# 64-row score tiles for the first head group, a new load order and a new last block in an attention and feed-forward kernel

## The chip, the cores and the metric

One core of one Trainium2 chip. The metric is the time of one execution in device microseconds. An execution more than 1.5% above the fastest of the same kernel is called slow here, and two kernels are compared by their fast executions alone, with a 95% interval. This matters more than usual: the kernel before has two times, some 921 and some 940 us, in about equal shares. Its executions near 921 us are called undisturbed below, those near 940 us disturbed.

## The reference

An input x (2048 rows, 512 columns, bfloat16) goes through attention with 32 heads of 16 elements and through a gated feed-forward block with 1792 hidden columns. A sigmoid gate for each row mixes the two.

```
g = sigmoid((x * gate_w).sum(-1, keepdims=True))
a = softmax(q @ k.T * 16 ** -0.5) @ v      # for each of 32 heads, then @ wo
b = (silu(x @ w_gate) * (x @ w_up)) @ w_down
out = g * a + (1 - g) * b
```

## The kernel before

Scores are kept transposed: 128 keys on the partitions, 512 queries along the row. Four heads make a group; there are 8 groups, 4 query blocks and 16 key tiles, so 2048 score tiles. Nearly all go in pairs to one 128x1024 exponential on ScalarE (902 of these); 244 single tiles get an approximate exponential on VectorE. "Pair n" below is the n-th exponential on ScalarE: a ruler that does not depend on time.

The four heads of a group lie at partitions 0, 32, 64 and 96. In group 0 a score is one 32-row matmul in its own row strip of the array. In the other groups it is a 64-row matmul over a strip of two heads, and the other head's rows of the query tile are zero:

```python
    HEADS = (0, 2, 1, 3)

    def score(ps, b):
        n, j = b // 4, HEADS[b % 4]
        (qb, g), kt = UNIT[n // KT], n % KT
        if g == 0:
            r = slice(32 * j, 32 * j + 32)
            mm(ps, lhsT=kaug[r, g, kt * P:(kt + 1) * P], rhs=q0[qb][r, :], start=True, stop=True,
               tile_position=(32 * j, 0))
        else:
            r = slice(64 * (j // 2), 64 * (j // 2) + 64)
            mm(ps, lhsT=kaug[r, g, kt * P:(kt + 1) * P], rhs=get_qx(qb, g // 2)[r, j % 2, g % 2, :],
               start=True, stop=True, tile_position=(64 * (j // 2), 0))
```

The query block of group 0 is made like this: a copy, the absolute value, a bound (one matmul), and its addition. `later(t, f)` and `plan.dve` do not run on the chip: they are the builder's estimates of when VectorE will be done, and by them it decides in which order the instructions are emitted.

```python
        def end():
            vec.tensor_copy(out=q0[qb], in_=st["p"][:, :])
            m_free(plan.dve)
            aq = work.tile([P, QBW], BF16, tag="aq", name="aq", bufs=4)
            vec.tensor_scalar(out=aq[:, :].bitcast(U16), in0=q0[qb].bitcast(U16), scalar1=0x7FFF, scalar2=None,
                              op0=ALU.bitwise_and)
            plan.dve += 0.33
            st["aq"] = aq

        def bound():
            st["b"] = m_tile("bp")
            mm(st["b"][:, :], lhsT=kneg0, rhs=st["aq"][:, :], start=True, stop=True)
            spend("F", 1)
            later(0.6, end_b)

        def end_b():
            vec.tensor_tensor(out=q0[qb], in0=q0[qb], in1=st["b"][:, :], op=ALU.add)
            m_free(plan.dve)
```

At the start the transposed input comes on SyncE's queue and the weights on ScalarE's. VectorE fills seven groups of `kaug` with ones before it can make the first key bound:

```python
    for c0 in (0, D):
        nc.scalar.dma_start(out=wqk[:, :, c0 + 64:c0 + D],
                            in_=A_wqkv[:, c0 + 64:c0 + D].rearrange("(dc p) c -> p dc c", p=P))
    # ... (cut)
    nc.scalar.dma_start(out=wv, in_=A_wqkv[:, 2 * D:3 * D].rearrange("(dc p) c -> p dc c", p=P))
    # ... (cut)
    for g in range(1, G):
        nc.vector.memset(kaug[:, g, :], 1.0)
```

At the end both halves of the last product wait for the last group's sums, and the four output tiles share two buffers (`opool` has `bufs=2`):

```python
    for w in range(2):
        for tq in range(TQ):
            cs = slice(tq * P, (tq + 1) * P)
            mm(a_ps[tq][:, 0:D], lhsT=(osbs[un - 1], on_l)[w][:, cs], rhs=wo_l[:, w, :],
               start=(w == 0), stop=(w == 1))
    for tq in range(TQ):
        store(qb * TQ + tq, a_ps[tq], acc[0][:, tq, :])
```

## Time and profile before

| | us |
|---|---|
| three timed executions | 921.09, 940.65, 945.73 (median 940.65) |
| profiled execution | 947.81, span 946.1, a slow one |
| ScalarE busy in the span | 876.4 (93%) |
| TensorE busy in the span | 856.0 (90%) |

The page of the kernel before cuts the span into 40 slices of 23.7 us. A digit is a share in tenths; PEclk is the clock granted to TensorE.

```profile
ACT  1989966899999999999999999999999999999994
PEclk9999855899999999999999999999999999999998
```

The two dips lie in the same slices. The timeline of the kernel before (start, duration, engine, idle before and who ended it):

```profile
57.38 0.40 PE L158 MATMUL s_t<-on,kaug 32*128 32x512 bf16 x4
57.61 0.37 PE L158 MATMUL d_t<-on,kaug 32*128 32x512 bf16 x1
57.90 1.94 ACT L161 ACTIVATE e_t<-s_t 128x1024 bf16<-128x1024 f32 x2 [0.57 <-PE s_t L158]
57.92 1.04 PE L158 MATMUL vp<-rb,xT 128*128 128x512 bf16 x4
```

Behind four value sums, for which it waited on VectorE's copy of a value tile, TensorE sends five scores in a row. From the first score to the next full matmul pass 57.92 - 57.38 = 0.54 us. ScalarE waits at its end for these scores: 0.57 us. Here TensorE is on the path, though it idles beforehand.

### The profile page before, as it was taken

How to read it: one execution, taken by the hardware profiler on the slowest of the kernel's cores; microseconds unless marked ns; L12 is line 12 of the kernel's file. 1: busy time of each engine (PE TensorE's matmuls, PEld its weight loads, DVE VectorE, ACT ScalarE, POOL GpSimd, SP SyncE). 2: the span in 40 equal slices, each digit the busy share in tenths (PEclk: the TensorE clock that was granted, in tenths of full speed). 3: DMA queues.
4: the chain of work that ended last, by engine and by line, in shares of the span. 5: the costliest groups of instructions: out<-in, count | busy, mean ns of one | idle time of the engine just before them, and what ended most of it. 6: DMA issues, size and time to landing. Idle time of an engine off the chain costs nothing.

```text
span 946.1 us, 14215 instructions
## 1 busy us (share of the span) xinstructions
PE 856.0 (90%) x5165; PEld 217.0 (23%) x5165; DVE 737.5 (78%) x1018; ACT 876.4 (93%) x967; POOL 8.9 (1%) x30
## 2 busy tenths in 40 slices
PE   4889999999999999999999998999999999889985
PEld 1222211222222222222222222222222222222221
DVE  7259865789888887987878778888778798887782
ACT  1989966899999999999999999999999999999994
POOL 3000000000000000000000000000000000000000
PEclk9999855899999999999999999999999999999998
DMA  9400102102110111111001112110001121100000
GB/s 182 112 4 19 30 18 40 35 21 53 27 29 7 35 37 41 53 45 33 7 4 29 37 33 53 46 38 13 4 12 32 39 56 35 29 9 4 23 1 22
DMA packets 87534, 31.97 MB, mean 34 GB/s; under 512 B 75120, under 2 KB 87016, under 8 KB 87464
## 3 DMA queue, kind: packets, MB, share of 16 engines
q1 hardware_dynamic: 84824, 29.50, 13.7%
q10 hardware_dynamic: 2640, 1.57, 0.7%
q8 instruction: 40, 0.66, 0.3%
q14 instruction: 30, 0.25, 0.1%
HBM read 20.83 MB, written 2.34 MB: 24 GB/s over the span
## 4 chain that ended last, share of the span: by engine, by line
PE 44%; ACT 38%; issue 10%; DVE 6%; DMA 2%; SPq 1%; ACTq 0%; DVEq 0%
ACT e_t L161 36%; PE s_t L158 17%; PE o_ps L158 9%; PE gp L158 4%; PE dps L158 3%; PE d_t L158 3%; PE up L158 2%; DVE y_t L167 2%; ACT th L161 2%; PE kp L158 2%; PE qp L158 1%; DMA xT<-in_A_x_dram 1%; PE a_ps L158 1%; PE vp L158 1%; DVE u_t L167 1%
## 5 line engine op out<-in xcount | busy, mean ns | idle before, releaser
L161 ACT ACTIVATE e_t<-s_t 128x1024 bf16<-128x1024 f32 x902 | 849.7, 1041 | 35.4 <-PE s_t L158 31.5
L158 PE MATMUL s_t<-qx,kaug 64*128 64x512 bf16 x1572 | 332.2, 386 | 54.9 <-ACT e_t L161 51.7
L167 DVE TENSOR_SCALAR y_t<-d_t 128x512 uint16<-128x512 f32 x244 | 167.6, 687 | 100.0 <-PE d_t L158 97.8
L158 PE MATMUL o_ps<-e_t,vaug 128*32 128x512 bf16 x1804 | 198.0, 398 | 4.6 <-DVE vaug L167 3.9
L158 PEld LDWEIGHTS <-kaug 64*128 64x128 bf16 (+1 forms) x2048 | 100.6, 93 | 358.3 <-issue 353.7
L167 DVE TENSOR_TENSOR u_t<-u_t,z_t 128x2048 f16<-128x2048 f16 x122 | 148.9, 1220 | 2.3
L158 PEld LDWEIGHTS <-vaug 128*32 128x32 bf16 x2048 | 53.3, 94 | 192.0 <-issue 183.4
L158 PE MATMUL d_t<-qx,kaug 64*128 64x512 bf16 x220 | 83.7, 380 | 0.0
L167 DVE TENSOR_TENSOR y_t<-y_t,u_t 128x2048 uint16<-128x2048 uint16 x61 | 74.4, 1219 | 0.8
L158 PE MATMUL gp<-xT,wg 128*128 128x512 bf16 x224 | 71.2, 401 | 0.0
L158 PE MATMUL up<-xT,wu 128*128 128x512 bf16 x224 | 70.0, 399 | 0.0
L158 PE MATMUL dps<-wd_t,mt 128*128 128x512 bf16 x224 | 67.6, 384 | 0.0
L158 PE MATMUL s_t<-on,kaug 32*128 32x512 bf16 x232 | 49.5, 443 | 3.8 <-ACT e_t L161 3.5
L167 DVE SCALAR_TENSOR_TENSOR mt<-gs,up 128x512 bf16<-128x512 bf16 x56 | 38.2, 682 | 14.6 <-PE up L158 13.9
L167 DVE SCALAR_TENSOR_TENSOR gs<-th,gp 128x512 bf16<-128x512 bf16 x56 | 38.1, 680 | 9.1 <-ACT th L161 8.8
L167 DVE TENSOR_SCALAR u_t<-z_t 128x2048 f16<-128x2048 uint16 x61 | 42.1, 691 | 1.5
L167 DVE TENSOR_SCALAR z_t<-y_t 128x2048 uint16<-128x2048 uint16 x61 | 41.9, 687 | 0.8
L167 DVE TENSOR_SCALAR u_t<-u_t 128x2048 f16<-128x2048 f16 x61 | 41.8, 686 | 0.7
L167 DVE TENSOR_SCALAR y_t<-y_t 128x2048 uint16<-128x2048 uint16 x61 | 41.8, 686 | 0.5
L161 ACT ACTIVATE th<-gp 128x512 bf16<-128x512 f32 x56 | 34.2, 610 | 0.3 <-PE gp L158 0.3
L167 DVE CAST osb<-o_ps 128x512 bf16<-128x512 f32 x32 | 21.9, 685 | 13.7 <-PE o_ps L158 13.5
L158 PEld LDWEIGHTS <-mt 128*128 128x128 bf16 x260 | 16.5, 100 | 52.6 <-issue 45.8
(89 smaller groups left out, 331.5 us busy)
## 6 DMA issues: line engine op xcount, KB each, us to landing
wg<-in_B_w_gate_dram SPq DMA_DIRECT2D x56, 128.0 KB
wu<-in_B_w_up_dram SPq DMA_DIRECT2D x56, 128.0 KB
out_dram<-o_t SPq DMA_DIRECT2D x16, 128.0 KB
on<-osb SPq DMA_DIRECT2D x120, 16.0 KB
rb<-rr SPq DMA_DIRECT2D x15, 128.0 KB
wd_t<-in_B_w_down_dram SPq DMA_DIRECT2D x1, 1792.0 KB
qx<-qst SPq DMA_DIRECT2D x112, 16.0 KB
kaug<-on SPq DMA_DIRECT2D x20, 64.0 KB
```

The costliest lines, as they stand in the source:

```text
L158: ordered(nc.tensor.matmul(*args, **kw))
L161: ordered(nc.scalar.activation(*args, **kw))
L167: return lambda *a, **kw: ordered(f(*a, **kw))
```

## The change

Its intent: give group 0 the 64-row form of the other groups; keep the weights from competing with the transposed input; shorten the last block. The 64-row form needs two query tiles with alternate heads zeroed (`vsel`), so VectorE passes over each block twice, and the bound takes two matmuls. The tiles borrow parts of other tiles (`qx`, `on_t`, `mt`). The order of emission has a new cap, at most two blocks of vector exponentials in flight (`y_live`), and a rule on late blocks; the planning charges were raised as well. The core of the diff:

```diff
-    for c0 in (0, D):
-        nc.scalar.dma_start(out=wqk[:, :, c0 + 64:c0 + D], ...)
-    nc.scalar.dma_start(out=wv, ...)
+    nc.sync.dma_start(out=wv, ...)          # behind the transposes on the same queue
+    for c0 in (D, 0):
+        nc.sync.dma_start(out=wqk[:, :, c0 + 64:c0 + D], ...)
 ... query block of group 0
-                    later(0.6, end)
+                    later(1.2, end)
-            vec.tensor_copy(out=q0[qb], in_=st["p"][:, :])
+            for v in range(2):
+                vec.tensor_scalar(out=q0[qb][:, v, :], in0=st["p"][:, :], scalar1=vsel[:, v:v + 1], scalar2=None,
+                                  op0=ALU.mult)
-            plan.dve += 0.33
+            plan.dve += 0.46
-            mm(st["b"][:, :], lhsT=kneg0, rhs=st["aq"][:, :], start=True, stop=True)
-            spend("F", 1)
-            later(0.6, end_b)
+            for v in range(2):
+                mm(st["b"][:, :], lhsT=kneg0, rhs=st["aq"][:, v, :], start=(v == 0), stop=(v == 1))
+            spend("F", 2)
+            later(1.2, end_b)
-            vec.tensor_tensor(out=q0[qb], in0=q0[qb], in1=st["b"][:, :], op=ALU.add)
+            for v in range(2):
+                vec.scalar_tensor_tensor(out=q0[qb][:, v, :], in0=st["b"][:, :], scalar=vsel[:, v:v + 1],
+                                         in1=q0[qb][:, v, :], op0=ALU.mult, op1=ALU.add)
 ... score(): the 32-row branch goes
+        r = slice(64 * (j // 2), 64 * (j // 2) + 64)
+        q = q0[qb][r, j % 2, :] if g == 0 else get_qx(qb, g // 2)[r, j % 2, g % 2, :]
 ... rules of emission
-        if late and (now is None or late[0][0] <= now):
+        if late and late[0][1][0] // (4 * KT) == closed and (now is None or late[0][0] <= now):
-            d_ok = dq and dq[0] <= pq[0][-1] + 2 and ...
+            d_ok = (vcur or y_live[0] < 2) and dq and dq[0] <= pq[0][-1] + 2 and ...
 ... last block
+    last_mm(0, osbs[un - 1])                # ahead of the wait for the last group
     dt = ps_d.tile([P, QBW], F32, tag="d", name="dt")
 ... (cut)
+    last_mm(1, on_l)
     for tq in range(TQ):
-        store(qb * TQ + tq, a_ps[tq], acc[0][:, tq, :])
+        store(qb * TQ + tq, a_ps[tq], acc[0][:, tq, :], mt[:, tq, :])
```

## The prediction

> **What bounds the kernel now.** I read the page's clock row first, then the busy times by stretch, the waits inside the odd stretch, the groups, and last the two ends in order of time.
>
> The three timed runs of before are 921.09, 940.65 and 945.73 us, so the median is not the kernel's only time. The clock row has a dip near the start; busy times by stretch (span; then PE, weight loads, VectorE, ScalarE, GpSimd as us and count; clock; DMA share; GB/s) show it:
>
> ```profile
> 100.00:105.00 5.00, 5.00 (x31) 1.44 (x30) 4.96 (x8) 5.00 (x7) 0.00 (x0) 1.00 0.24 53
> 105.00:110.00 5.00, 3.97 (x36) 1.32 (x34) 4.86 (x8) 5.00 (x7) 0.00 (x0) 0.98 0.12 28
> 110.00:115.00 5.00, 5.00 (x20) 0.81 (x19) 2.76 (x5) 3.61 (x5) 0.00 (x0) 0.50 0.00 1
> ...
> 170.00:175.00 5.00, 5.00 (x17) 0.74 (x15) 1.73 (x3) 3.47 (x4) 0.00 (x0) 0.54 0.11 26
> 175.00:180.00 5.00, 5.00 (x34) 1.19 (x33) 4.97 (x8) 4.56 (x7) 0.00 (x0) 1.00 0.24 54
> ```
>
> Outside that stretch ScalarE is the bound: 98.5 of every 100 us from 200 to 900 us. Inside it TensorE has half its clock, is busy all the time, and ScalarE starves. The waits from 109.7 to 174.6 us (total, times, longest):
>
> ```profile
> ACT e_t L161 <- PE s_t L158: 20.9, 28, 1.9
> ```
>
> The page's groups say what runs there: 232 first-group score tiles of 32 rows, slower in the mean than the 64-row ones (386 ns):
>
> ```profile
> L161 ACT ACTIVATE e_t<-s_t 128x1024 bf16<-128x1024 f32 x902 | 849.7, 1041 | 35.4 <-PE s_t L158 31.5
> L158 PE MATMUL s_t<-on,kaug 32*128 32x512 bf16 x232 | 49.5, 443 | 3.8 <-ACT e_t L161 3.5
> ```
>
> So 20.9 of ScalarE's 35.4 us of idle before exponentials lie in the half-clock stretch. The profiled run (947.81 us) is a slow one; 940.65 - 921.09 = 19.6 and 945.73 - 921.09 = 24.6 say that the 921.09 run simply missed the dip.
>
> The start, in order of time (start, duration, engine, idle before and its releaser):
>
> ```profile
> 15.51 1.86 PE L158 MATMUL kp<-xT,mt 128*128 128x512 bf16 x4 [6.75 <-DMA xT<-in_A_x_dram]
> 17.43 1.76 DVE L222 MEMSET kaug<- 128x2048 bf16 x1 [0.38 <-issue]
> 20.90 1.23 DVE L167 TENSOR_REDUCE kpart<-kp 128x1 f32<-128x1024 f32 x1 [1.68 <-PE kp L158]
> 24.94 1.08 ACT L161 ACTIVATE vaug<-vp 128x512 bf16<-128x512 f32 x2
> 25.58 1.02 PE L158 MATMUL vp<-rb,xT 128*128 128x512 bf16 x4 [2.21 <-ACT vaug L161]
> 28.21 17.52 ACT L161 ACTIVATE e_t<-s_t 128x1024 bf16<-128x1024 f32 x19
> ```
>
> TensorE waits 6.75 us for transposed input, but VectorE has memsets until 17.43 + 1.76 = 19.19 us and reaches the reduction only behind them. The end:
>
> ```profile
> 939.27 1.41 DVE L167 SCALAR_TENSOR_TENSOR o_t<-al,gval,kaug 128x512 bf16<-128x512 f32 x2 [1.78 <-PE al L158]
> 941.90 1.41 DVE L167 SCALAR_TENSOR_TENSOR o_t<-a_l,gval,kaug 128x512 bf16<-128x512 f32 x2 [1.22 <-DMA out_dram<-o_t]
> ```
>
> The third and fourth output tiles wait 1.22 us for the first stores to free their buffer.
>
> [...] the half-clock stretch is 64.853 us, 19 windows of 3.413 us. [...]TensorE was busy 2.80 of the 3.4 us before the drop, and fully busy while held down[...]. I counted, for each window on the trace's own grid, rows x columns x streamed elements of the matmuls that start in it, over 128 x 128 x 8192[...]. A 512-element 32-row score, or a 128-row 32-column value matmul, is 1/4 x 1/16 = 0.0156; a 64-row score 0.031; a full one 0.0625. The window that ends at the drop (106.3 to 109.7) has 8 scores, 8 value matmuls, one full one and small ones: 0.125 + 0.125 + 0.0625 + 0.005 = 0.317, the lowest of all in the stage. The held windows have 0.27 to 0.375 and the one before release 0.406. From 175 to 932 us the lowest is 0.406 and the clock never drops; at 932 us a window of 0.127 drops it. One threshold between 0.375 and 0.406 fits every transition. That is my estimate from the trace[...]. [...] here a pair of scores takes about 0.39 us in either shape, as only two run side by side, so 64 rows should cost no time.
>
> **The change part by part.**
> 1. 64-row first group. Recounting the bad window with 64 rows gives 0.317 + 8 x 0.0156 = 0.442, above the threshold. The changed instruction order also spreads that spot: by the same count over four successive score pairs (4 x 0.92 us), before has a minimum of 0.207 at pair 78, after 0.438 anywhere in the first 250 pairs. So the drop should go in every run: -20.9 us of starvation, less about 1 us of ordinary idle, -20 us against a slow run, nothing against the 921.09 run.
> 2. Its price. Three more 128-row bound matmuls, 3 x 0.22 = 0.7 us of TensorE. On VectorE each of three later query blocks goes from one 0.69 us copy and 0.29 us mask to two 0.69 us products and a mask twice as wide (about 0.46), and from one 0.69 us addition to two: 3 x (0.86 + 0.69) = 4.7 us, spread over 28 to 75 us. VectorE waited 19.4 us for value tiles there, so it is hidden: 0. The first block's halves are separate instructions and the first score pair waits for the first half only: 0 to 0.7.
> 3. Weights behind the input. Input packets moved 1800 per 2 us when alone and about 560 beside the weights; 8192 packets at 900 per us need 9 us, so the last quarter lands near 12 rather than 19.6 us and the projections end near 14.5. But the memsets remain: VectorE starts its first reduction at about 19.9, against 20.90: -0.9. Against that, TensorE now idles from about 17 to 24 us, over two windows, and resumes at half clock: four value matmuls and the bound on the path cost 5 x 0.21 = 1.1 us more, and one or two windows of slow start perhaps 1 us. Net +1.2 (-1 to +3).
> 4. The end. Four matmuls of the earlier group go ahead of the wait for the last group's sums, into 0.79 us in which TensorE idles: the first output tile can start about 1.2 us earlier; the stores from own tiles drop the 1.22 us wait. Together -2.4.
> 5. The emission rules (a cap on vector-computed blocks in flight) reorder but do not add: after has the same 902 exponentials and, in its order, the same runs of four value-tile matmuls ahead of value sums that cost ScalarE 3.3 us at 52 to 63 us. 0 +/- 3.
>
> Sum: 921.1 + 1.2 - 2.4 = 919.9. The profiled run less its excess gives 946.1 - 20 = 926 instead; since that run was also 4.6 us above the mean of the two slow timed ones, it points to about 921 and so the same. I take 920.
>
> **The rivals.**
> - The clock still drops, elsewhere. Against: 64-row windows before never fell under 0.406 until the end; for: 0.406 is only just above what held the clock, and the reordered stages are new. A drop with 64-row tiles would recover in a few windows, each about 3.4 x 0.3 = 1 us: 922 to 926. If it stays as long as before, 940.
> - Activity is not what I count, and the drop comes from the short pauses of TensorE just before it (0.6 us of 3.4) alone. Then the rearranged order decides; the time would be 920 or 940 by chance.
> - The start gains in full: if the memsets do not hold the reduction, the input's 7 us come through: 914. Against it stands the row that ends at 19.19.
> - The doubled VectorE work delays the query blocks and stalls scores near 40 to 70 us, where ScalarE already lost 3.3 us: 923 to 925.
>
> **Range and chances.** With the drop gone the base is 921 +/- 3; start and end add -4 to +1, order +/- 3: 913 to 928 for 8 in 10. Two per cent under 940.65 is 921.84, so a predicted 920 sits barely past it: faster 0.57, same 0.41 (nearly certain if only the undisturbed run of before is compared), slower 0.02.
>
> **What would show it.** The clock row should be full from about 30 us to the end; no 32-row group; score matmuls near 385 ns throughout; ScalarE's idle before exponentials near 15 us in place of 35.4; the input landed by 13 us, yet the first exponential still at 27 to 30 us, behind memsets and at half clock; no wait for stores at the end. The prediction is wrong if a half-clock stretch appears between 30 and 900 us, if the first exponential moves by more than 3 us, or if ScalarE idles over 15 us from 200 to 900 us.

Passages of the forecast that rest on no trace are cut, and the cuts are marked. They take no term out of its sum: 921.1 + 1.2 - 2.4 = 919.9. What it uses of the traces:

- A window is 3.413 us, the length of the shortest clock records in the trace of before (half clock from 935.78 to 939.19 us, full from 939.19 to 942.60). The three longer records before them, of 88.747, 64.853 and 761.172 us, are 26, 19 and 223 times that; the first three of after, of 10.240, 6.827 and 894.292 us, are 3, 2 and 262 times. The divisor of the count only scales it: 16 full matmuls of 512 elements, which start 0.215 us apart at full clock, fill about one window.
- That the count sets the clock, with a threshold between 0.375 and 0.406, is the author's estimate from the one trace of before, and so is the "activity theory" in the expectations below.
- The half clock of step 3 is an estimate too. In before, behind TensorE's idle 6.75 us, matmuls start 0.43 us apart from 15.89 us, as they had before it (from 6.44), and 0.215 apart from 21.05 on; the first full-clock record begins at 21.01. At the end a record of half clock follows the window from 939.19 to 942.60 us, in which TensorE is busy 0.51 us.
- The wider mask of step 2, put at 0.46 us (an estimate), took 0.43 in the trace of after. The input: at most 1823 of its 8192 packets start within 2 us in the trace of before, and 549 per 2 us in the mean from 8 to 14 us, where the weights' packets run beside them; in after 1619 to 1726 per 2 us from 4 to 12 us.

## The result, and the profile after

The changed kernel took 925.62, 927.82, 925.57 and 927.77 us, median 926.69. The kernel before had one more execution beside it, 921.20 us, which puts its median of four at 930.92: two fast, two slow. A ratio here is of one kernel's fast runs to the other's beside it, so it is not quite the ratio of these medians. It is 1.0057 [1.0035, 1.0079]: after is about 0.6% slower than an undisturbed before, and that is under 2%. The time lies in the predicted range (913 to 928), 6.7 us above the predicted 920; the favoured outcome, faster by over 2%, did not come.

The page of the changed kernel, its clock row and the groups that answer to those of before:

```profile
PEclk9999999999999999999999999999999999999999
...
L161 ACT ACTIVATE e_t<-s_t 128x1024 bf16<-128x1024 f32 x902 | 848.5, 1043 | 19.6 <-PE s_t L158 15.0
L158 PE MATMUL s_t<-qx,kaug 64*128 64x512 bf16 x1692 | 353.8, 383 | 56.5 <-ACT e_t L161 50.4
```

The clock row is full, no 32-row group is left, and ScalarE's idle time before exponentials is 19.6 us against 35.4 in the slow execution of before. The busy times of after in the stretch where before's clock fell:

```profile
105.00:110.00 5.00, 4.81 (x47) 1.43 (x46) 4.83 (x7) 4.95 (x7) 0.00 (x0) 1.00 0.02 5
110.00:115.00 5.00, 4.60 (x36) 1.36 (x34) 4.90 (x8) 4.79 (x7) 0.00 (x0) 1.00 0.06 13
```

ScalarE is busy 4.79 of 5 us from 110 to 115 us, where before had 3.61. So the clock stayed full where the forecast said that it would; whether for the reason that it gave is tested below. The start of after, in order of time:

```profile
12.70 1.02 PE L158 MATMUL kp<-xT,mt 128*128 128x512 bf16 x4 [0.64 <-DMA xT<-in_A_x_dram]
...
16.76 1.76 DVE L228 MEMSET kaug<- 128x2048 bf16 x1 [0.38 <-issue]
18.45 1.21 DVE L167 TENSOR_REDUCE kpart<-kp 128x1 f32<-128x1024 f32 x1
23.12 1.86 PE L158 MATMUL vp<-rb,xT 128*128 128x512 bf16 x4 [6.76 <-ACT vaug L161]
27.39 1.94 ACT L161 ACTIVATE e_t<-s_t 128x1024 bf16<-128x1024 f32 x2
```

The last key projection starts at 12.70 us; in before it starts at 19.81, and the line at 15.51 that the forecast shows is the second of four. The reduction comes behind the last fill, at 18.45; in before it came at 20.90 and waited for TensorE's projections at the end (1.68 us), not for the fills. TensorE idles 6.76 us, and the four matmuls after it take 1.86 us in place of 1.02: the clock records of this trace show half clock from 19.65 to 26.47 us. The first exponential starts at 27.39 us (28.21 in the trace of before). The end of after:

```profile
918.43 1.41 DVE L167 SCALAR_TENSOR_TENSOR mt<-al,gval,kaug 128x512 bf16<-128x512 f32 x2
919.76 1.40 DVE L167 SCALAR_TENSOR_TENSOR mt<-a_l,gval,kaug 128x512 bf16<-128x512 f32 x2
```

The second pair of output tiles follows 1.33 us after the first, without the wait for a store (2.63 us in before). From the start of the last exponential to the end of the span: 13.0 us before, 9.8 after.

Where did the rest go? By the ruler of pairs (us, from the traces):

| stretch | before | 64 rows, before's order | after | predicted difference |
|---|---|---|---|---|
| start to pair 0 | 28.2 | 25.7 | 27.4 | +1.2 |
| pairs 0 to 25 | 22.90 | 23.29 | 23.78 | 0 to 0.7 |
| pairs 25 to 80 | 56.14 | 60.40 | 58.80 | 0 |
| pairs 80 to 130 | 74.22 (half clock) | 49.12 | 49.72 | -20 in slow runs, else 0 |
| pairs 130 to 901 | 751.57 | 751.68 | 754.38 | 0 +/- 3 |
| pair 901 to the end | 13.0 | 13.0 | 9.8 | -2.4 |

The middle column is the first experiment. An undisturbed before is not traced; if its pairs 80 to 130 take 49.1 us like those of the middle column, which is assumed, after loses 0.9 + 2.7 + 0.6 + 2.8 = 7.0 us in the stream and gains 3.2 at the end. That leaves +3.8 of the measured 0.57% (5.3 us); the other 1.5 us are left to the start, which differs from run to run (below), and to scatter; no run shows them.

### The profile page after: what moved, and what is told of

The parts are those of the page before. It is cut to its first block, busy times and chain, and to the rows that moved or that the text cites. A ratio compares the mean times of both kernels' runs of the same rounds, so it can differ in the third digit from the quotient of the medians.

```text
span 923.9 us, 14142 instructions
## 1 busy us (share of the span) xinstructions
PE 819.3 (89%) x5073; PEld 219.1 (24%) x5168; DVE 744.2 (81%) x1032; ACT 874.4 (95%) x967; POOL 7.1 (1%) x29
## 4 chain that ended last, share of the span: by engine, by line
PE 40%; ACT 39%; issue 11%; DVE 9%; ACTq 0%; DMA 0%; DVEq 0%
ACT e_t L161 37%; PE s_t L158 16%; PE o_ps L158 9%; DVE y_t L167 4%; PE dps L158 3%; PE d_t L158 3%; PE gp L158 3%; PE up L158 2%; ACT th L161 2%; DVE kaug L228 1%; PE kp L158 1%; PE qp L158 1%; PE vp L158 1%; DVE u_t L167 1%; PE a_ps L158 1%
## 5 line engine op out<-in xcount | busy, mean ns | idle before, releaser
L161 ACT ACTIVATE e_t<-s_t 128x1024 bf16<-128x1024 f32 x902 | 848.5, 1043 | 19.6 <-PE s_t L158 15.0
L158 PE MATMUL s_t<-qx,kaug 64*128 64x512 bf16 x1692 | 353.8, 383 | 56.5 <-ACT e_t L161 50.4
L158 PE MATMUL o_ps<-e_t,vaug 128*32 128x512 bf16 x1804 | 192.9, 389 | 7.9 <-DVE vaug L167 4.6
L158 PEld LDWEIGHTS <-kaug 64*128 64x128 bf16 x2048 | 103.2, 93 | 345.4 <-issue 339.1
L158 PE MATMUL d_t<-qx,kaug 64*128 64x512 bf16 x228 | 85.7, 376 | 0.0
L158 PE MATMUL dps<-wd_t,mt 128*128 128x512 bf16 x201 | 62.6, 384 | 3.0 <-issue 3.0
L158 PE MATMUL up<-xT,wu 128*128 128x512 bf16 x203 | 62.7, 384 | 2.4 <-issue 2.4
L158 PE MATMUL gp<-xT,wg 128*128 128x512 bf16 x198 | 62.0, 384 | 2.1 <-issue 2.1
L158 PE MATMUL o_ps<-y_t,vaug 128*32 128x512 bf16 x244 | 24.5, 389 | 5.8 <-DVE y_t L167 5.1
```

The lines of the kernel that those rows point to most:

```text
L158: ordered(nc.tensor.matmul(*args, **kw))
L161: ordered(nc.scalar.activation(*args, **kw))
```

## The experiments

Eighteen runs, in groups by question. "R" in a diff is the kernel that the run is made from. base_again, base_look and rules_ref repeat a kernel; the others change one or a few parts. Times of pairs are given beside the whole times, since these also hold the scatter of the start.

### Is the drop of the clock the kernel's or the chip's?

**base_again** and **base_look**: the kernel before, unchanged.

> The kernel before, unchanged. Wanted: its trace in the undisturbed state and how often the half-clock stretch comes. If the stretch depends only on how the 3.413 us window grid lies over the one poor spot near score pair 78, some runs have it and some do not: times near 921 and near 940 to 946, nothing between. My accounting says an undisturbed trace should reach score pair 130 about 24.5 us earlier than the slow one and span about 919.5 us; if the span is 921.5, the timed 921 runs must differ elsewhere too.

> The kernel before once more, for a trace in the undisturbed state (about 4 in 10 runs). If it is undisturbed: span near 919.2 us, first exponential at 25.5 to 28.2 us, 12 to 13 us after the last one, so about 880 us between, against 884.5 in rows64_before_order and 886.7 in the changed kernel; and its lead over rows64_before_order lies in pairs 25 to 120. If 12 to 13 us at the end is wrong in this state, the end's gain of 3 us is not one against undisturbed runs.

base_again: 1677.21, 944.87, 920.83, 943.64 us. base_look: 943.93 and 922.45. Counting every execution of before, 33 of 68 took 918.6 to 923.0 us, 34 took 934.7 to 948.0, and one took 1677.21. The trace of base_look has its half-clock stretch from 109.14 to 167.16 us, nearly where the first trace had it, so this is a place in the program and not a moment of the chip. The 1677 us execution is something else. Its trace has no clock records; a row of its page:

```profile
L158 PE MATMUL s_t<-qx,kaug 64*128 64x512 bf16 x1572 | 603.7, 697 | 8.8 <-ACT e_t L161 5.9
```

A 64-row score took 697 ns in the mean in place of 386, from start to end of the execution. I have no cause for it; it enters no comparison.

### Which part of the change keeps the clock?

**rows64_before_order**: 64 rows, with the loads, the end, the planning charges and the emission rules of before.

```diff
 R = after
-+ loads on SyncE, last_mm early, own store tiles, later(1.2), y_live cap
+  all of these as in before
```

> 64-row first group alone, with the emission order, loads and stores of before (TensorE order the same but for three more bound matmuls). Activity theory: no half-clock stretch of 19 windows in any run, since the held-down windows recounted with 64 rows lie at 0.34 to 0.44 and 0.406 released the clock; at most a dip of 1 to 4 windows at pair 78 (count over four pairs 0.322), costing 1 to 4 us; so 921 to 926 in all runs. Rival, the order alone removed the stretch: runs near 940 appear as often as before. On cost: if the 5 us that the changed kernel loses against the fast runs of before come from the 64-row shape (pairs no longer run four wide, doubled VectorE passes), this one is at 924 to 927 in the fast state; if they come from the reordering, it is at 921 to 922.5.

926.53 us median, 924.9 to 926.91, ratio 1.0057 [1.0042, 1.0073], full clock from 18.5 to 912.8 us. So the 64-row part alone keeps the clock, and it alone reproduces the loss against an undisturbed before.

**after_rows32**: the converse.

```diff
 R = after, in score()
+        if g == 0: r = slice(32 * j, 32 * j + 32), rhs=q0[qb][r, j % 2, :], tile_position=(32 * j, 0)
```

> The changed kernel with 32-row score matmuls put back, in its own order, loads and stores, so that only the rows of 256 matmuls differ. Activity theory: the counts over four pairs have minima of 0.362 at pairs 64 and 102, just under the threshold, and a window once held down cannot rise over 0.375, so some or all runs are at half clock for a long stretch and take 938 to 950; runs without it take 923 to 926. Rival, the order alone: never a stretch, 923 to 926 in all runs. On cost: if the 64-row shape costs in the stalls at 49 to 65 us, an undisturbed run here is 1 to 2 us faster than the changed kernel.

931.73, 938.5, 926.47, 932.54, 938.72, 937.23 us; the trace has half clock from 100.84 to 117.91 us. The drop is back, shorter in this trace and, to judge by the times, in most of the others; the granted clock of the six is 0.971 to 0.989, against 0.991 to 0.995 in after.

**rows32_masks**: 32-row scores, but everything else of rows64_before_order, so the doubled VectorE passes in before's order.

```diff
 R = rows64_before_order, the same edit in score()
```

> The doubled VectorE passes (masked copies, wide mask, two-step bound) with 32-row score matmuls, in the order, loads and stores of before: only the rows of 256 matmuls differ from rows64_before_order. It sorts the 4 us that the 64-row kernel loses between score pairs 25 and 80. Theory VectorE: the doubled passes cost it, so pairs 25 to 80 take about as long as in rows64_before_order (60.4 us; 56.1 in before) and undisturbed runs take 924 to 926. Theory four-wide: two score pairs back to back take 0.2 us less with 32 rows, which feeds each stall, so pairs 25 to 80 take 56 to 57.5 us and undisturbed runs 921 to 922.5. Between the two, a split. Activity theory, for the drop: with the poor spot back at pair 78 (0.207), runs with a long half-clock stretch come again, near 936 to 948.

945.12 us median, and all six executions disturbed (940.26 to 954.53 us, granted clock 0.953 to 0.973; no execution of a 64-row kernel at ordinary speed is under 0.990). The clock row of its page:

```profile
PEclk9995785899999999999999999999999999999998
```

Two half-clock stretches, 68.56 to 109.52 and 136.83 to 174.38 us. This kernel and rows64_before_order differ only in the shape of group 0's scores: six of six against none of six. So in this order the shape decides. It is not alone: against before, which is 32 rows too, the doubled passes and bound matmuls raise the disturbed executions from a half to six of six, and in after_rows32 the drop is shorter. The loads and the end don't remove it (loads_tail below has three disturbed of six).

### Is it my count of activity?

The forecast explained the drop by rows x columns x streamed elements in a window. **fill128** leaves before as it is and adds full 128x128 matmuls, overwritten at once by the score, where that count is lowest.

```diff
 R = before, in emit_pair()
+    FILL = set(range(68, 73)) | set(range(76, 84)) | set(range(88, 93)) | set(range(105, 110))
+        if pairs[0] in FILL:
+            mm(s_t[0:128, 0:QBW], lhsT=xT[:, 0, 0:128], rhs=xT[:, 0, 0:QBW], start=True, stop=True)
```

> The kernel before, 32-row tiles and all, with 23 extra matmuls of 128 rows and 128 columns written into score tiles and overwritten by the scores, at the poor spots of the first stage (pairs 68-72, 76-83, 88-92, 105-109). The count over four pairs then has a minimum of 0.438 (0.207 in before). If array activity is what releases or holds the clock, no run has the long half-clock stretch: all six at 920 to 924, the fillers' 23 x 0.216 = 5 us of TensorE partly hidden. If the 32-row shape or anything else of it is the cause, runs near 936 to 946 appear as in before (about 5 or 6 in 10). It also gives an undisturbed 32-row trace: pairs 80 to 130 should take 49 to 51 us (49.1 with 64 rows).

926.35 us median, all six undisturbed (925.48 to 926.99), ratio 1.0048 [1.0033, 1.0063]. As the count says. But the control, **fill1**, has the same matmuls with one column in place of 128, so nearly nothing is added to the count. (In the trace of before a 512-element matmul takes as long with few columns as with 128: 379 ns with 8, 384 with 128, in the median.)

```diff
-            mm(s_t[0:128, 0:QBW], lhsT=xT[:, 0, 0:128], ...
+            mm(s_t[0:1, 0:QBW], lhsT=xT[:, 0, 0:1], ...
```

> The control: the same 23 extra matmuls at the same places, of the same 512 columns streamed and so the same TensorE time, but with one stationary column each, so that they add 1/128 of the activity (minimum over four pairs 0.208). Activity theory: the long stretch stays, in about half of the runs or more, 936 to 950. Rival, TensorE's idle pauses trip it: the fillers close these pauses as in fill128, and the stretch goes here too.

925.18 us median, also all six undisturbed (923.9 to 926.33). Two rows of its page:

```profile
PEclk9999999999999999999999999999999999999997
...
L158 PE MATMUL s_t<-on,kaug 32*128 32x512 bf16 x232 | 43.0, 383 | 2.6 <-ACT e_t L161 2.3
```

The 32-row scores themselves run at 383 ns and the clock stays. By my count over four pairs fill1 has a minimum of 0.208, before 0.207, after 0.438. So the count as I made it is not the cause, or not alone. The traces say so more directly. Counted as in the forecast, by the matmuls that start in each window of the trace's own grid, fill1 has a window of 0.257 (105.5 to 109.0 us), loads_tail one of 0.317 (104.9 to 108.3) and rows32_masks one of 0.317 (123.2 to 126.6), and the clock stays full behind each of them; in base_look it falls behind one of 0.380. These traces have a record of every matmul. So no single threshold fits them, though one fits the trace of before. Nor do TensorE's pauses within a window sort them: the clock fell behind a window with 2.81 us busy in before, and stayed behind one with 1.85 us in loads_tail (50.3 us); and in before it stayed at half from 130 to 174.6 us with TensorE busy 45.00 of 45 us (130 to 175). What the fillers share is that TensorE pauses less (from 105 to 110 us it is busy 4.67 us in fill1, 3.97 in before) and streams 128 rows once more. What sets the clock stays open: fill1 was meant to separate width from presence, and I have no run that separates rows from pauses.

### What do 64 rows cost?

**cheapmask** has 64 rows and TensorE's order of before, but copies, bounds and adds once and makes the two masked tiles only afterwards.

```diff
 R = rows64_before_order, end() and end_b()
-            for v in range(2): tensor_scalar(out=q0[qb][:, v, :], in0=st["p"], scalar1=vsel ...)
+            vec.tensor_copy(out=qs[:, :], in_=st["p"][:, :])
-            for v in range(2): scalar_tensor_tensor(out=q0[qb][:, v, :], in0=st["b"], scalar=vsel ...)
+            vec.tensor_tensor(out=st["q"][:, :], in0=st["q"][:, :], in1=st["b"][:, :], op=ALU.add)
+            for v in range(2):
+                vec.tensor_scalar(out=q0[qb][:, v, :], in0=st["q"][:, :], scalar1=vsel[:, v:v + 1], ...)
```

> 64-row first group in the order, loads and stores of before, with the masks applied once, after the bound has been added, from SBUF: 0.69 + 0.29 + 0.69 + 0.61 = 2.3 us of VectorE per later query block in place of 3.25 (before 1.67), and one bound matmul as before; the TensorE order is that of before exactly. Theory VectorE: recovers most of the loss, fast runs at 921.5 to 923, pairs 25 to 80 in 57 to 58 us. Theory four-wide: recovers 1 us at most, 924 to 925.5. Activity theory: no long half-clock stretch in any run.

924.18 us median (923.18 to 925.07), ratio 1.0035 [1.002, 1.005]. Pairs 25 to 80 take 58.32 us: 2.1 less than rows64_before_order and still 2.2 more than before. The first difference is VectorE's, with a small part of TensorE's: cheapmask also saves the second bound matmul (0.38 us in place of 0.59 below). The timeline of before, where a query block is made:

```profile
65.34 0.69 DVE L167 CAST on<-qp 128x512 bf16<-128x512 f32 x1 [1.03 <-PE qp L158]
...
66.41 0.38 PE L158 MATMUL bp<-aq,mt 128*128 128x512 bf16 x1 [0.45 <-DVE aq L167]
...
67.21 3.77 ACT L161 ACTIVATE e_t<-s_t 128x1024 bf16<-128x1024 f32 x4 [0.19 <-PE s_t L158]
```

And the timeline of rows64_before_order at the same place of the program:

```profile
64.27 1.41 DVE L167 TENSOR_SCALAR on<-qp,vsel 128x512 bf16<-128x512 f32 x2 [1.04 <-PE qp L158]
...
66.19 0.59 PE L158 MATMUL bp<-mt 128*128 128x512 bf16 x2 [1.10 <-DVE mt L167]
...
67.20 2.86 ACT L161 ACTIVATE e_t<-s_t 128x1024 bf16<-128x1024 f32 x3 [1.27 <-PE s_t L158]
```

The bound waits for the copies and the absolute value, 1.41 + 0.43 us in place of 0.69 + 0.29; TensorE stands 1.10 us in place of 0.45; and the score pair behind the bound in TensorE's order comes late, so that ScalarE idles 1.27 us in place of 0.19. Work on VectorE that I called hidden is on the path here, through TensorE's order of instructions. In cheapmask pairs 35 to 40 take 4.88 us, as in before (4.86), against 5.94 in rows64_before_order. Its masks, from VectorE's groups between 53 and 82 us, are cheaper as well: from bfloat16 in SBUF they take 350 ns each (0.70 us for two, where 0.61 was expected), from float32 in PSUM 745 in rows64_before_order:

```profile
L167 DVE TENSOR_SCALAR on<-mt,vsel 128x512 bf16<-128x512 bf16 x4 | 1.2, 350 | 0.1
```

Most of the other 2.2 us is TensorE's. The same burst as the one shown of before, in the timeline of after:

```profile
60.74 0.60 PE L158 MATMUL s_t<-qx,kaug 64*128 64x512 bf16 x4
61.19 0.38 PE L158 MATMUL d_t<-qx,kaug 64*128 64x512 bf16 x1
61.23 1.94 ACT L161 ACTIVATE e_t<-s_t 128x1024 bf16<-128x1024 f32 x2 [0.96 <-PE s_t L158]
61.50 1.04 PE L158 MATMUL vp<-rb,xT 128*128 128x512 bf16 x4
```

Five scores take 61.50 - 60.74 = 0.76 us to the next full matmul, against 0.54 with 32 rows. Without the fifth it is 0.54 against 0.33 (54.90 to 55.23 us in before). So four 32-row scores do overlap, and four of 64 rows take one slot of 0.21 us more. Pairs 25 to 35 hold five such bursts and measure 13.06 us in before, base_look, loads_tail and rows32_masks (all 32 rows, in before's order), and 14.1 in every kernel of 64 rows at ordinary speed: 5 x 0.21 = 1.05.

The other 1.1 us lie in pairs 40 to 80, and there single pairs cost more as well. Pair 47 in the timeline of before:

```profile
74.91 0.39 PE L158 MATMUL s_t<-on,kaug 32*128 32x512 bf16 x2
```

And in that of cheapmask:

```profile
75.48 0.60 PE L158 MATMUL s_t<-qx,kaug 64*128 64x512 bf16 x2
```

The order of heads puts the two scores of a pair into different strips. But the vector exponentials take single heads out of it, and by the program's list of pairs the two heads of pairs 34, 37, 44, 47, 62, 65, 72 and 75 then share one 64-row strip. In cheapmask the second score of each of these that stands alone starts 0.22 to 0.23 us behind the first; in before it starts beside it, for there every head has a strip of its own. At or just behind pairs 47, 62 and 72 cheapmask falls another 0.2 us behind the kernel before, together 0.6 us. One more step of 0.2 us, at pair 53, is a wait of TensorE for VectorE (0.23 us). The last 0.3 us are not traced.

### What is the new order of emission worth?

**rows64_rules**: rows64_before_order with the cap and the rule on late blocks. (The converse, after without them, was not run.)

> rows64_before_order with the change's cap on vector-computed blocks in flight, planning costs as before. The changed kernel needs 886.7 us from first to last exponential, rows64_before_order 884.5. If the cap costs this, 886 to 887 us here and 0.2 per cent more time (927.5 to 928.5); if the planning costs do (they move most of the first stage), 884 to 885 us and 926 to 927.

925.34 us median, ratio 1.0046 [1.0026, 1.0067]; pairs 130 to 901 take 751.98 us. The rules cost 0.3 us. What is left is the planning charges. **rules_ref** is the same kernel again, as the base on one chip for two runs that change one part each: **rules_plan** the charges, **rules_end** the end.

```diff
 R = rules_ref                                rules_plan
-                    later(0.6, end)           +  later(1.2, end)
-            plan.dve += 0.33                  +  plan.dve += 0.46
-            spend("F", 1); later(0.6, end_b)  +  spend("F", 2); later(1.2, end_b)
 R = rules_ref                                rules_end
-    last product and stores as in before      +  last_mm early, stores from mt[:, tq, :]
```

> The same kernel as rows64_rules (64-row first group, the cap on vector-computed blocks, but before's planning charges, loads and end), again, as the base on this chip for the two runs beside it: 925.3 plus or minus 1 us, undisturbed in all executions, ratio 1.0046 plus or minus 0.002.

> rules_ref with the changed kernel's planning charges alone (later 1.2 for 0.6, 0.46 for 0.33, two bound matmuls charged for one). If the new order of emission costs what subtraction gave, score pairs 130 to 901 take 754.4 us in place of 751.98 and pairs 0 to 80 about the same or 1 us less, and the time rises by 2 to 3 us, to 927.5 to 928.5. The rival: the order alone is worth nothing (under 1 us) and the 2.4 us came from the loads or the end reaching back into the stream.

> rules_ref with the new end alone (early matmuls of the earlier group, four stores from own tiles). If the traces' shorter end is the whole story, the time falls by 3.0 to 3.3 us, to about 922.2. The rival, which loads_tail left open: the end is worth only about 0.7 us in time, to about 924.6, because something outside the traced span or the start takes the rest.

rules_ref: 927.73 us median, ratio 1.0067 [1.0053, 1.008]. It is 2.4 us above rows64_rules, the same kernel: the traces put 1.6 of it at the start, where the first exponential comes at 27.42 against 25.86 us.

rules_plan: 930.25 us median, ratio 1.0091 [1.0072, 1.0109]. The means, 930.0 against 927.6 us, differ by 2.4 us, by the scatter of the two sixes 0.6 to 4.2. Pairs 25 to 80 gain (58.80 us against 60.39), the rest loses. Pairs 130 to 901 take 755.60 us, which contains one half-clock window. The other traces with these charges have 754.38 to 754.57 us there, those without 751.45 to 752.40; the rival, that the order alone is worth nothing, falls. The window, in busy times by stretch:

```profile
367.00:370.50 3.50, 3.50 (x18) 0.71 (x15) 2.62 (x5) 2.54 (x3) 0.00 (x0) 0.52 0.00 0
```

Only three exponentials start in it. The clock can fall with 64-row tiles too, then, and one window cost ScalarE 3.50 - 2.54 = about 1 us.

rules_end: 924.77, 926.27, 923.95, 923.38, 923.45 us, ratio 1.0029 [1.0014, 1.0044], so 3.2 us less between the means of the fast runs (924.4 against 927.6 us). The end is worth in time what the traces say. Its profiled execution took 1359.68 us, again without clock records and with 559 ns for a score: the second of these whole-execution anomalies, in another kernel.

### Are the loads and the end worth anything?

**after_oldloads**: after with the weights on ScalarE's queue again. **loads_tail**: before with the new loads and the new end.

```diff
 R = after                                   after_oldloads
-    nc.sync.dma_start(out=wv, ...)           +  nc.scalar.dma_start(out=wv, ...)
 R = before                                  loads_tail
-    loads and last block of before           +  loads and last block of after
```

> The changed kernel with the weight loads on their old queue, same order on TensorE. My prediction's step: the early input gains about 1 us by an earlier reduction and loses 1 to 2 us by a cold start, so this one should have its first exponential at 28 to 28.9 us (0.5 to 1.5 us later), no half-clock windows between 20 and 27 us, and take 925.5 to 927.5. Rival, the cold start costs more than the trace of one run shows (runs at 927.8 us have more half-clock time): it takes 923 to 925 and its runs agree within 0.5 us.

> The kernel before with the moved loads and the new end, still 32-row tiles and the order of before. By the traces the end gains 3.2 us (12.0 to 8.8 us after the last exponential) and the loads nothing (after_oldloads against the changed kernel: 926.1 to 926.7). So undisturbed runs at 917 to 919, disturbed ones at 933 to 944. If the gain at the end is real in the time, the 64-row part and the reordering together cost 7 to 8 us against it; rival, the end gains nothing in the time, and undisturbed runs stay at 920 to 922.

after_oldloads: 926.12 us median, ratio 1.0059 [1.0044, 1.0074], against 1.0057 of after: the loads are worth nothing that these runs can tell. Its first exponential starts at 27.59 us. With the old loads the first exponential came anywhere from 25.67 to 28.53 us in the traces, according to where the half-clock windows fall (the two traces under 26 us have full clock from 18.3 and 18.5 us on); with the new ones, behind the same fills, at 27.2 to 27.8.

loads_tail: three fast runs, 919.73, 920.19, 920.76 us, ratio 0.9992 [0.9973, 1.0012]; the other three slow. Its trace ends in 9.85 us like after, so 3.2 less, but only 0.7 us show. Pairs 130 to 901 take 0.8 us more than in base_look, and the start may hold the rest: fast executions of before are not traced. That stays open in size.

### Does moving the fills free the start?

**after_gpmemset** has GpSimd do the seven fills.

```diff
 R = after
-    for g in range(1, G):
-        nc.vector.memset(kaug[:, g, :], 1.0)
+    for g in range(1, G):
+        nc.gpsimd.memset(kaug[:, g, :], 1.0)
```

> The changed kernel with the seven large fills of the key tile moved from VectorE to GpSimd, nothing else. My step 3 said that these fills, not the input, hold the first reduction (18.45 us in the changed kernel, with the projections done at 13.9). If so: first reduction at 14.0 to 14.5, first exponential at 20.5 to 22.5 instead of 27.4, TensorE without the half-clock windows at 19.7 to 26.5 (idle for 2 to 3 us only), and a time 5 to 7 us shorter: 919 to 921. If the reduction then waits for something else (input, weights), less than 2 us.

927.12 us median, ratio 1.0065: nothing gained. Its timeline at the start:

```profile
7.90 12.27 POOL L410 MEMSET kaug<- 128x2048 bf16 x7
...
13.15 1.22 DVE L167 TENSOR_REDUCE kpart<-kp 128x1 f32<-128x1024 f32 x1 [6.92 <-PE kp L158]
...
14.41 5.82 DVE L167 TENSOR_SCALAR mt<-mt,kpart 128x128 bf16<-128x128 bf16 x1
```

The reduction now starts at 13.15 us in place of 18.45. But the next small product takes 5.82 us, where it takes 0.25 in after, and ends at 20.23 when GpSimd's fills end (7.90 + 12.27 = 20.17). The absolute value behind it, 0.29 us in after, takes 5.78 and ends at 20.35. The reduction ahead of it, also beside the fills, takes 1.22 us, as in after (1.21). So in this trace two VectorE instructions were held until GpSimd's fills ended and the reduction was not; what makes the difference is not shown.

**after_splitfill** gives GpSimd only three fills, which should be done before VectorE comes to the small product.

```diff
-    for g in range(1, G):
+    for g in range(1, 5):
         nc.vector.memset(kaug[:, g, :], 1.0)
+    for g in range(5, G):
+        nc.gpsimd.memset(kaug[:, g, :], 1.0)
```

> The changed kernel with the seven fills of the key tile split, four on VectorE and three on GpSimd, so that both are done when the projections end. In after_gpmemset the reduction did start at 13.15 us, but VectorE's next small operation took 5.82 us, until GpSimd's seventh fill ended at 20.17. If that block is what replaced the wait, here: no VectorE operation of several us after 13.5, first exponential at 20 to 22.5 us, no half-clock windows before it or one, and the time 5 to 7 us below the changed kernel: 919.5 to 921.5. Rival: the start is held by something further (weights, cold clock), then 924 or more.

926.23, 919.28, 920.54, 920.28, 921.08, 919.03 us: five of six some 6 us below after. In the 926.23 us run, the profiled one, a VectorE copy at 6.32 us was blocked for 6.95 us until the fills ended at 13.16, and the gain was lost. GpSimd's long fills had begun at 6.13 us. In the trace of best2 (below), which has the same split, this copy starts at 5.79, ahead of them, and takes 0.26 us. So in these two traces it is decided by which engine comes first; the five faster executions are not traced.

### A version that beats both

**best2**: 64 rows with cheapmask's late masks, before's order, the new loads, the new end and the split fills. **fill128_ends**: fill128 with the same loads, end and fills.

> 64-row first group with late masks in the order of before (cheapmask), the moved loads, the new end and the split fills. Sum from traces: 881.9 us from first to last exponential (cheapmask), 20.5 to 22 at the start, 9.8 to 10.9 at the end: span 912 to 915, time 914 to 917, no half-clock stretch, faster than the fast runs of before (920.9) by 0.4 to 0.8 per cent and 2 per cent or more under its slow ones.

> fill128 with the moved loads, the new end and the fills split between VectorE and GpSimd: the 32-row rival of best2. If 32 rows are worth about 3 us of the first stage and the fillers cost 1 to 3, it takes 912 to 916 in all runs, about as best2 (915.1); if VectorE is blocked at the start by GpSimd's fills (two more of them are ahead here), 917 to 921.

best2: 915.1 us median (914.88 to 916.94), all six undisturbed, ratio 0.9942 [0.9921, 0.9963] to the fast runs of before; every run is below every run of both kernels. fill128_ends: 918.04 us, ratio 0.9958 [0.9943, 0.9973]. The start of best2:

```profile
13.05 1.22 DVE L167 TENSOR_REDUCE kpart<-kp 128x1 f32<-128x1024 f32 x1
...
17.73 1.02 PE L158 MATMUL vp<-rb,xT 128*128 128x512 bf16 x4 [0.75 <-ACT vaug L161]
...
20.36 1.94 ACT L161 ACTIVATE e_t<-s_t 128x1024 bf16<-128x1024 f32 x2
```

With the fills out of the way the reduction starts at 13.05 us and the first exponential at 20.36, 7.0 us before after's. TensorE's pause shrinks from 6.76 to 0.75 us, and the four matmuls behind it run at full clock. Here the earlier input pays at last.

## Why the prediction was right and wrong

The forecast of 920 says a gain of 1.1 us on the undisturbed 921.1; measured is a loss of 5.3. Step 2 failed: over pairs 0 to 80, where the price was put at 0 to 0.7 us, after loses 3.5 us. Step 5 was mis-sized: another 2.8 us. That the time still lies in the range owes something to its width, and to an end that gained 0.8 us more than was forecast.

1. **64-row first group: the outcome right, the reason given for it not borne out, its weight misjudged.** None of 63 executions of 64-row kernels at ordinary speed fell to the long half-clock stretch (the 64th is the 1359.68 us one), while about half of before's did. "-20 us against a slow run" is -24.5 in the traces (74.22 to 49.72 us for pairs 80 to 130). I counted only ScalarE's idle time; exponentials without a neighbour also lose their overlap, 1.02 us each against a pitch of 0.92. The reason, a count that crosses a threshold between 0.375 and 0.406, failed in fill1 and in the windows of three other traces (0.257 and 0.317 with the clock kept, 0.380 with a drop). So it is partly luck that the outcome was right. And "nothing against the 921.09 run" was right and decisive: the comparison is between fast runs. I gave "faster" 0.57 because a median of three happened to be a slow run.
2. **Its price: wrong.** "here a pair of scores takes about 0.39 us in either shape, as only two run side by side, so 64 rows should cost no time" failed. It is true of pairs over two strips, but not of the bursts of four, 0.33 against 0.54 us, and not of the pairs that share a strip, 0.39 against 0.60, on ScalarE's path: 1.05 and 0.6 of 2.2 us. "So it is hidden: 0" for VectorE failed too: the bound, and the score behind it, wait for the added passes, 2.1 us in before's order (60.40 against 58.32 in cheapmask). In after the raised planning charges put the bound later (TensorE stands 0.53 us before it in place of 1.10) and win most of that back (58.80). I took VectorE's 19.4 us of idle as room, but there it was waiting for TensorE, on the same chain. The rival "923 to 925" named this.
3. **Weights behind the input: right in kind.** Input landed early, the fills held the reduction, and TensorE, after 6.76 us of idling, resumed at half clock (four matmuls in 1.86 us, in place of 1.02). The reduction came 2.45 us earlier (20.90 to 18.45) and not 0.9, for before's had waited for the projections. Predicted +1.2 (-1 to +3); after_oldloads says about 0.
4. **The end: right, a little small.** -2.4 predicted; -3.2 in the traces, -3.2 in time by rules_end, though only 0.7 show in loads_tail.
5. **The emission rules: mis-sized.** "Reorder but do not add ... 0 +/- 3" was +2.8 over pairs 130 to 901 of after, inside the range, but the order does add; rules_plan shows +2.4 us in time from the planning charges alone. I looked at the cap, which costs 0.3, and not at the charges.

The activity count of the prediction fitted the trace that it was made from and no more: fill1 removes the drop without raising it. That the shape decides in before's order is shown; by what measure is not. Two small slips of the working: TensorE was not quite "fully busy while held down" (64.15 of 64.90 us), and 946.1 - 20 starts from the span, where the time was 947.81.

## What to carry to other kernels

Look at all timed executions before taking a median as the base: what removed a slow state here (24.5 us) gained nothing on a fast run, and its side costs then decided. Ask what a shape costs where the instructions stand in bursts on the path, and whether two that should run side by side ever fall on the same strip (0.60 us against 0.39 here); and look whether an engine that idles is waiting on the chain that the new work lengthens (VectorE waited 19.4 us for value tiles here, and 2.1 us of its new work still showed). A builder's planning charges are part of a change: they alone moved 2.4 us here.
